# Output weights moved from the first MLP pass into gaps of the projections' plan, and half of the T forms put in the places of the token forms

## The chip, the cores and the metric

The kernel runs on one core of a Trainium2 chip. The time is device microseconds (us) of one execution. The engines are PE (TensorE, with PEld for its weight loads), DVE (VectorE), ACT (ScalarE), POOL (GpSimd) and SP (SyncE, which issues the DMAs here). Each works through its own queue of instructions in order.

## The reference

For 2048 tokens of 640 numbers, the result is the input, plus a linear attention of its layer norm, plus an MLP of its layer norm:

```python
xn = _layernorm(x)
return x + _A_ref(xn, A_wqkv, A_w_phi, A_wo) + _B_ref(xn, B_w1, B_b1, B_w2, B_b2)

# _A_ref: 32 heads of 20
q, k, v = split(x @ wqkv)
pq, pk = q @ w_phi, k @ w_phi                    # per head
phi = concat(softmax(p), softmax(-p))            # for q and for k
kv, z = phi_k^T @ v, sum over tokens of phi_k
o = (phi_q @ kv) / (phi_q @ z + 1e-6)
return o @ wo
# _B_ref
return gelu(layernorm(x) @ w1 + b1) @ w2 + b2    # 640 -> 1728 -> 640
```

## The kernel before

All matmuls work on pairs of numbers. A float32 operand is split into a high part (an ACT copy that rounds it) and a low part (the rest, by a subtract on POOL or DVE), and a product is three matmuls: high by high, high by low, low by high (`mm3`, lines 68 to 71). Tokens come in four blocks `b` of 512, hidden units in 14 chunks of 128, taken in seven groups `g` of two.

The stages in order of time, by the trace: the first MLP pass over blocks 0 and 1 for all groups, up to about 225 us; then the projections of q, k and v with the feature maps and phi_k^T v, up to about 447 us; then the MLP over blocks 2 and 3 with the attention beside it; then the product with `wo`.

**The first pass** (`Mlp.passes`) runs, for each group and block, the first layer (two chunks, 30 matmuls), then the second layer of the pass before it (five columns of 6 matmuls, each read out of its bank by a DVE add, L338). Between two passes the next weight chunk is split (`take`; L60 on ACT, L63 on POOL or DVE; the last, half-wide chunk 13 by L60, L63 and L271 to L275). After every 3 matmuls `Mlp.tick` runs one step of a generator, `beside`. In this pass that is `prep()`, which prepares what later stages read. Its last part is a list of `events`, each a tick number and a step, sorted by tick. An event says when a step is written into its engine's queue; there it runs when what stands before it is done and its data are there. The events of before:

- For the ten tiles (c, b) of the tokens of blocks 2 and 3 (c of 5 rows of 128, b of 2 blocks): `load` of a 128x512 tile `xq` (four buffers; L795), `centred` on POOL at tick +0 (L798), `scaled` on DVE at +3 (L801), `hi` on ACT at +5 (L805) and `lo` on DVE at +7 (L809). `hi` and `lo` write the two halves of a tile `t`, of which there are two buffers; two DMAs store them (L811). The tiles follow each other every 5 ticks.
- *Token forms* (`form_sub` on POOL L835, `form_hi` on ACT L839, `form_lo` on DVE L843, stores L846): differences of halves of tiles, for a scheme that saves matmuls in the projections. For block 2 they lie in `temps[:4]`, four 128x512 pieces of the memory of `acc2`: the forms in the first two, their high parts in the other two.
- *T forms* (`combine` on POOL L821, then `hi`, L805, and `combined_lo` on DVE L826, with one store of 512 KB, L827): differences of tiles, four for each `q` in (0, 1), for a like scheme in the later MLP. They use the same two buffers `t`.
- *Output weights* (`wo_load` L855, `wo_hi` on ACT L858, `wo_lo` on POOL L861 with two stores L863): the first 512 of the 640 columns of `wo`, in five blocks `kc` of 128 rows, at ticks 46, 49, 52, 97 and 100, with `wo_hi` 8 and `wo_lo` 10 ticks later. They lie in `temps`, `spare` and `own["t"]`.
- `raw_sums` from tick 122 (DVE L918, POOL L921): sums of weight blocks in `temps`.

DVE, ACT, POOL and PE keep the order in which the program writes their instructions. SP's order is chosen by the framework.

**The projections** are written by a planner, `Plan` (from line 1200). Each `add` names an engine, a duration, a function that emits the instructions, and what must be done before. `run()` places the operations one after another, each at the earliest time by its priority, and emits an operation when it is placed. `plan_pair` plans two tiles of 128 tokens; inside, `plan_wo` (L1529) plans the last 128 columns of `wo` in three parts, each a load, an ACT copy (L1541), a POOL subtract (L1544) and stores (L1548). `next_forms` loads 1 MB of token forms for the next pair (L1197). `store_phi` stores turned features (L1178) from five places `turns`, which are used in turn.

Of the kernel before, what the change touches and what calls it, by code (L numbers as in the profile page):

```python
# [8 lines left out]
F32 = mybir.dt.float32  # L9
F32R = mybir.dt.float32r  # L10
AF = mybir.ActivationFunctionType
ALU = mybir.AluOpType
# [3 lines left out]
P = 128  # L16
S, D, F, H, DH = 2048, 640, 1728, 32, 20
KC = D // P
# [27 lines left out]
def f(ap):  # L46
    return ap.bitcast(F32)
# [3 lines left out]
def tile_kernel(ctx: ExitStack, tc: tile.TileContext, x, xT, wkT, wqT, wv, wphi, wo, w1, b1, w2, b2,  # L51
# [715 lines left out]
    def prep():  # L767
# [32 lines left out]
        def scaled(c, b):  # L800
            nc.vector.tensor_tensor(xs[c, b], xs[c, b], mr[b][:, 1], op=ALU.mult)  # L801

        def hi(*at):
            hls[at] = gp.tile([P, 2, 512], F32R, name="t")
            nc.scalar.activation(hls[at][:, 0], xs[at], AF.Copy)  # L805

        def lo(*at):
            hl = hls.pop(at)
            nc.vector.tensor_tensor(hl[:, 1], xs[at], f(hl[:, 0]), op=ALU.subtract)  # L809
            for p in range(2):  # L810
                nc.sync.dma_start(y_dram[at[1] - 2][p][:, at[0], :], f(hl[:, p]))  # L811
# [11 lines left out]
        def combined_lo(q, i):  # L823
            at = combined(q, i)[0]
            hl = hls.pop(at)
            nc.vector.tensor_tensor(hl[:, 1], xs[at], f(hl[:, 0]), op=ALU.subtract)  # L826
            nc.sync.dma_start(t_dram[q][:, i], f(hl))  # L827

        def form_sub(b, q, i):
            w = 512 if b == 2 else 2 * P  # L830
# [20 lines left out]
        wos = {}  # L851

        def wo_load(kc):
            wos[kc] = [(temps[0], temps[1]), (temps[2], temps[3]), (spare[0], own["t"])][kc % 3]
            nc.sync.dma_start(wos[kc][0], wo[kc * P:(kc + 1) * P, :512])  # L855

        def wo_hi(kc):
            nc.scalar.activation(wos[kc][1].bitcast(F32R), wos[kc][0], AF.Copy)  # L858

        def wo_lo(kc):  # L860
            nc.gpsimd.tensor_tensor(wos[kc][0].bitcast(F32R), wos[kc][0], wos[kc][1], op=ALU.subtract)  # L861
            for w, wd in zip(wos[kc][::-1], wo_dram):
                nc.sync.dma_start(wd[:, kc, :512], w)  # L863

        for kc, at in enumerate((46, 49, 52, 97, 100)):
            for after, step in ((0, wo_load), (8, wo_hi), (10, wo_lo)):
                events.append((at + after, len(events), step, (kc,)))

        for n, step in enumerate(raw_sums(0, temps)):
            events.append((122 + 3 * n, len(events), step, ()))  # L870
        base = 8
        for q in range(3):
            tiles = [(c, b) for c in range(2 * q, min(2 * q + 2, KC)) for b in range(2, 4)]
            for n, at in enumerate(tiles):
                late = 6 * (at == (KC - 1, 3))
                for after, step in ((-6, load), (0, centred), (3, scaled), (5 + late, hi), (7 + late, lo)):
                    events.append((base + 5 * n + after, len(events), step, at))
            if q < 2:
                for b, at, his, los in ((2, 14, (25, 27), (27, 29)), (3, 19, (29, 31), (31, 33))):
                    for i in range(4):  # L880
                        events.append((base + at + i, len(events), form_sub, (b, q, i)))
                    for i in range(2):
                        events.append((base + his[i], len(events), form_hi, (b, q, i)))
                        events.append((base + los[i], len(events), form_lo, (b, q, i)))
            base += 5 * len(tiles) + (9 if q < 2 else 5)
            if q < 2:
                for n, i in enumerate((0, 2, 1, 3)):
# [312 lines left out]
    class Plan:  # L1200
# [31 lines left out]
            for op, t in zip(self.ops, last):  # L1232
                op[4] = t

        def run(self):

            self.latest()
            engines = ("PE", "ACT", "DVE", "POOL", "SP")
# [4 lines left out]
            rest = []  # L1243
            while any(left.values()):
                best = None
                for e, ops in left.items():
# [15 lines left out]
                op[0] = e  # L1262
                free[e] = op[5] = at + op[1][e]
                if left["PE"] or e == "PE":
                    op[2][e]()
# [125 lines left out]
        if (t, 1 - n) in got:  # L1391
            plan_features(t, "k", j, got[t, 0][0], got[t, 1][0])

    at, got, wo_done = {}, {}, []
    yts = {}

    def plan_pair(t):
# [78 lines left out]
    def next_forms(t):  # L1476
        if t < 12:
            yts[t + 2] = load_forms(t + 2)
        else:
            for q in range(2):  # L1480
                for p in range(2):
                    nc.sync.dma_start(f(wkv_[p][:, 2 * q, 512:1024]), s_dram[:, q, p])

    def plan_sums():
# [34 lines left out]
                late[1 + i][:] = way  # L1519

        done = splits(1, ts, ways1, (plan.add("ACT", 0.0, place, *done, *made),))
        w_ready["s1"] = (*w_ready["s1"], plan.add("SP", 3.5, lambda: next_forms(0), *done))
        return thirds

# [1 line left out]
        acc[2] = own["a"].tile([P, KC, 512], F32, name="acc2")  # L1526
        load_acc(2)

    def plan_wo(n, *after):  # L1529

        ks, cols = slice(2 * n, min(2 * n + 2, KC)), slice(512, D)
        raw = {}

        def load():
            r = rp.tile([P, D], F32, name="r2")
            w = (ks.stop - ks.start) * P
            raw.update(lo=r[:, :w], hi=r[:, 320:320 + w])
            nc.sync.dma_start(raw["lo"].rearrange("p (c n) -> p c n", n=P), wo[ks.start * P:ks.stop * P, cols].rearrange("(c p) n -> p c n", p=P))

        def hi():  # L1540
            nc.scalar.activation(raw["hi"].bitcast(F32R), raw["lo"], AF.Copy)  # L1541

        def lo():
            nc.gpsimd.tensor_tensor(raw["lo"].bitcast(F32R), raw["lo"], raw["hi"], op=ALU.subtract)  # L1544

        def store():
            for w, wd in zip((raw["hi"], raw["lo"]), wo_dram):
                nc.sync.dma_start(wd[:, ks, cols], w.rearrange("p (c n) -> p c n", n=P))  # L1548

        a = plan.add("SP", 0.7, load, *after, *wo_done)  # L1550
        b = plan.add("ACT", 0.4, hi, a)
        c = plan.add("POOL", 0.7, lo, b)
        wo_done[:] = [plan.add("SP", 1.4, store, c)]

    def first_weights():
        nonlocal mlp
# [30 lines left out]

    w1t = w2t = late = None
    w_ready = {}
    thirds = plan_sums()  # L1590
    for n, (t, i) in enumerate(((0, 0), (0, 1), (1, 1), (0, 2), (0, 3), (1, 0), (1, 2), (1, 3))):
        plan_part(t, i, n % 3)
# [23 lines left out]
    for b, op in stores:  # L1616
        for m in range(4):
            stored = plan.add("SP", 2.8, lambda b=b, m=m: store_phi(b, m), op, at[4 * b + 4, m] if b else op)
            if m < 3:
                turned[4 * b + 4][3] = (*turned[4 * b + 4][3], stored)  # L1620
    ptile.n = n
    over = plan.run()
    order.close()
    for step in over:
        step()
# [601 lines left out]
```

## Time and profile before

| | |
|---|---|
| median of three runs | 709.65 us |
| lowest and highest | 708.47 and 710.87 us |
| the profiled execution | 707.67 us |
| its span, first to last instruction | 705.9 us |
| mean granted PE clock | 0.995 |
| DMA | 123.37 MB, mean 175 GB/s |

A row of the profile names a line, an engine and an operation, what it writes and reads by the program's names, and times. A bracket such as `[3.18 <-DMA t<-t]` means that the engine was idle for 3.18 us before this instruction, and what ended it: here a DMA that read or wrote a tile `t`. "Granted clock" is the share of full speed at which PE ran. PE's matmuls overlap, so their lengths add up to more than the time they take.

### The profile page before, as it was taken

Reading aid. Unit: us, or ns where it says so; the run is one execution under the profiler, and the core shown is the slowest. Engines: PE = TensorE matmul, PEld = TensorE weight load, DVE = VectorE, ACT = ScalarE, POOL = GpSimd, SP = SyncE. Lnnn points to the kernel's source line nnn. Section 1 sums busy time; section 2 is a strip of 40 time slices with the busy share of each in tenths; the row PEclk is TensorE's granted clock in tenths of the full one; section 3 lists DMA queues with packets and bytes.
Section 4 is the critical chain, followed back from the end, with each engine's and each line's share of the span. In section 5 each row is a group of like instructions: output and inputs, shape, how many; then the busy total and the mean of one; then the engine's idle time right before and its main releaser. Section 6 shows DMA issues by size and latency. Waiting matters only on the chain.

```text
span 705.9 us, 9957 instructions
## 1 busy us (share of the span) xinstructions
PE 691.2 (98%) x3295; PEld 579.6 (82%) x3295; DVE 544.3 (77%) x912; ACT 376.6 (53%) x644; POOL 516.1 (73%) x390
## 2 busy tenths in 40 slices
PE   8999999997899999999999999999999999999997
PEld 7888888876677888888888888888888888888886
DVE  7878774877667788788888888848688697789783
ACT  6444564444343455455454465657677667659350
POOL 3717585879539779979979999848689997577930
PEclk9999999999989999999999999999999999999999
DMA  9815867597845213384370564984355648871222
GB/s 325 248 59 176 251 190 250 205 302 260 263 165 179 86 59 125 125 211 162 96 186 0 159 150 148 313 254 116 124 141 162 186 145 290 284 275 65 75 75 105
DMA packets 78202, 123.37 MB, mean 175 GB/s; under 512 B 8502, under 2 KB 41942, under 8 KB 75758
## 3 DMA queue, kind: packets, MB, share of 16 engines
q1 hardware_dynamic: 75670, 120.62, 53.4%
q10 hardware_dynamic: 2480, 2.11, 0.9%
q8 instruction: 26, 0.43, 0.3%
q14 instruction: 26, 0.21, 0.1%
HBM read 79.76 MB, written 42.94 MB: 174 GB/s over the span
## 4 chain that ended last, share of the span: by engine, by line
PE 82%; DVE 6%; DMA 5%; POOL 3%; issue 2%; ACT 2%; SPq 0%; DVEq 0%; POOLq 0%; ACTq 0%
PE bank L1044 17%; PE bank L69 15%; PE bank L71 15%; PE bank L70 15%; PE bank L1416 8%; PE bank L1157 3%; PE bank L1420 2%; PE bank L650 2%; POOL xq L798 1%; PE bank L1768 1%; PE bank L1769 1%; DMA t<-t 1%; DMA f<-xq 1%; PE bank L556 1%; DVE acc L843 1%
## 5 line engine op out<-in xcount | busy, mean ns | idle before, releaser
L69 PE MATMUL bank<-m,w 128*128 128x512 f32 x288 | 113.9, 396 | 3.7 <-DVE acc L338 3.7
L70 PE MATMUL bank<-m,w 128*128 128x512 f32 x288 | 112.4, 390 | 0.0
L71 PE MATMUL bank<-m,w 128*128 128x512 f32 x266 | 103.8, 390 | 0.0
L69 PE MATMUL bank<-y,w 128*128 128x512 f32 (+1 forms) x256 | 99.6, 389 | 0.0
L70 PE MATMUL bank<-y,w 128*128 128x512 f32 (+1 forms) x256 | 98.8, 386 | 0.0
L71 PE MATMUL bank<-y,w 128*128 128x512 f32 (+1 forms) x246 | 95.1, 387 | 1.2 <-POOL w L63 1.2
L63 POOL TENSOR_TENSOR w<-r,w 128x640 fp32r<-128x640 f32 x29 | 49.5, 1719 | 30.2 <-ACT w L60 25.6
L69 PEld LDWEIGHTS bank<-m,w 128*128 128x128 f32 x288 | 54.4, 189 | 17.3 <-DVE acc L338 5.7
L1044 PE MATMUL bank<-wkh,y 128*128 128x320 f32 (+1 forms) x240 | 63.1, 337 | 0.0
L70 PEld LDWEIGHTS bank<-m,w 128*128 128x128 f32 x288 | 54.2, 188 | 10.8
L71 PEld LDWEIGHTS bank<-m,w 128*128 128x128 f32 x266 | 50.1, 188 | 10.7
L1044 PE MATMUL bank<-w,y 128*128 128x512 f32 x240 | 57.5, 391 | 0.0
L69 PEld LDWEIGHTS bank<-y,w 128*128 128x128 f32 x256 | 48.1, 188 | 10.4 <-ACT bank L1836 0.3
L70 PEld LDWEIGHTS bank<-y,w 128*128 128x128 f32 x256 | 48.1, 188 | 9.5
L71 PEld LDWEIGHTS bank<-y,w 128*128 128x128 f32 x246 | 46.2, 188 | 11.1 <-POOL w L63 1.6
L338 DVE TENSOR_TENSOR acc<-bank,acc 128x512 f32<-128x512 f32 x70 | 46.4, 680 | 8.5 <-PE bank L334 5.0
L1762 POOL TENSOR_TENSOR e<-e,m 128x512 fp32r<-128x512 f32 x28 | 41.1, 1468 | 15.4 <-ACT m L1761 14.4
L1044 PEld LDWEIGHTS bank<-w,y 128*128 128x128 f32 x240 | 44.4, 188 | 8.5
L1097 POOL TENSOR_TENSOR m<-m,w 128x1280 f32<-128x1280 f32 x16 | 41.3, 2584 | 11.3 <-DVE w L1090 10.0
L1084 DVE TENSOR_REDUCE sm<-m 128x64 f32<-128x1280 f32 x32 | 47.1, 1472 | 2.9 <-ACT m L1079 2.6
L1138 ACT ACTIVATE v<-bank,rs_all 128x132 fp32r<-128x132 f32 (+2 forms) x48 | 19.6, 443 | 52.4 <-PE bank L1044 52.1
L1076 POOL TENSOR_TENSOR m<-m,mx 128x640 f32<-128x640 f32 x32 | 40.9, 1279 | 8.3 <-DVE mx L1066 4.1
(311 smaller groups left out, 1827.9 us busy)
## 6 DMA issues: line engine op xcount, KB each, us to landing
r<-in_w SPq DMA_DIRECT2D x52, 320.0 KB
e<-e SPq DMA_DIRECT2D x40, 256.0 KB
e<-acc SPq DMA_DIRECT2D x52, 160.0 KB
w<-f SPq DMA_DIRECT2D x6, 1024.0 KB
t<-t SPq DMA_DIRECT2D x8, 512.0 KB
acc<-in_xT SPq DMA_DIRECT2D x3, 1280.0 KB
tf<-t SPq DMA_DIRECT2D x2, 1536.0 KB
xb<-in_x SPq DMA_DIRECT2D x8, 320.0 KB
```

The source lines that it names most:

```text
L63: eng.tensor_tensor(lo, src, f(hi), op=ALU.subtract)
L69: nc.tensor.matmul(ps, lh, rh, start=first, stop=False, **kw)
L70: nc.tensor.matmul(ps, lh, rl, start=False, stop=False, **kw)
L71: nc.tensor.matmul(ps, ll, rh, start=False, stop=last, **kw)
L338: nc.vector.tensor_tensor(acc[b][:, m, :], pw, acc[b][:, m, :], op=ALU.add)
L1044: nc.tensor.matmul(ps, lh[:, kc, c], rh[:, kc], start=n == 0, stop=n == 3 * KC - 1)
L1076: subs[n, t] = nc.gpsimd.tensor_tensor(ep[:, :, s], a, b, op=ALU.subtract)
L1084: nc.vector.tensor_reduce(sm, e.rearrange("p a (h f) -> p (a h) f", f=DH), axis=AX, op=ALU.add)
L1097: nc.gpsimd.tensor_tensor(e3, e3, w.unsqueeze(2).to_broadcast([P, 2 * H, DH]), op=ALU.mult)
L1157: nc.tensor.matmul(kvp[g // 2][:, (g % 2) * 240:(g % 2) * 240 + 240].rearrange("p (i c) -> p i c", i=2), v[:, g * VS:(g + 1) * VS], ft[:, ...
L1416: nc.tensor.matmul(ps, left(yn, pl, q), right(w, pr, q), start=first and q == 0 and n == 0, stop=False, skip_group_check=True)
L1762: mlp.after(1, lambda: nc.gpsimd.tensor_tensor(pl, e, f(ph), op=ALU.subtract))
```

## The change

- The events of `wo` leave the first pass: five loads, ACT copies, POOL subtracts and pairs of stores.
- `plan_wo` leaves the plan. In its place five *pieces* (`wo_piece`), one for each block of 128 rows and all 640 columns, are placed after the plan is finished: `run()` first collects what it planned in `seq`, with times. Then, for each piece, it looks on each engine that a step may use for the first gap that is long enough after the step before it (SP is taken as free), and puts the step there; the subtract goes to POOL (1.9) or DVE (1.0), whichever can begin first. At the end all is emitted in order of planned time. The raw block lies in `r2`, its high part in a place of `turns` that isn't in use: the fifth, once the second set of sums is split, the fourth and third, after their features are stored.
- Of the four T forms of each `q`, the second and the fourth in order write into `temps[0:2]` and `temps[2:4]` rather than into a buffer `t`. All T forms are stored by two DMAs of 256 KB instead of one.
- Ticks: `scaled` at +4 instead of +3, `hi` at +7 instead of +5, `lo` at +9 instead of +7; the subtracts of the token forms one tick later.

```diff
-        def hi(*at):
-            hls[at] = gp.tile([P, 2, 512], F32R, name="t")
-            nc.scalar.activation(hls[at][:, 0], xs[at], AF.Copy)
+        def hi(*at, place=None):
+            hl = gp.tile([P, 2, 512], F32R, name="t") if place is None else place
+            hls[at] = [hl[:, p] for p in range(2)] if place is None else [z.bitcast(F32R) for z in place]
+            nc.scalar.activation(hls[at][0], xs[at], AF.Copy)
...
-            nc.sync.dma_start(t_dram[q][:, i], f(hl))
+            for p in range(2):
+                nc.sync.dma_start(t_dram[q][:, i, p], f(hl[p]))
...
-        for kc, at in enumerate((46, 49, 52, 97, 100)):
-            for after, step in ((0, wo_load), (8, wo_hi), (10, wo_lo)):
-                events.append((at + after, len(events), step, (kc,)))
...
-                for after, step in ((-6, load), (0, centred), (3, scaled), (5 + late, hi), (7 + late, lo)):
+                for after, step in ((-6, load), (0, centred), (4, scaled), (7 + late, hi), (9 + late, lo)):
...
-                for b, at, his, los in ((2, 14, (25, 27), (27, 29)), (3, 19, (29, 31), (31, 33))):
+                for b, at, his, los in ((2, 15, (25, 27), (27, 29)), (3, 20, (29, 31), (31, 33))):
...
-                    for after, step in ((0, combine), (3, lambda q, i: hi(*combined(q, i)[0])), (5, combined_lo)):
+                    place = temps[n - 1:n + 1] if n % 2 else None
+                    for after, step in ((0, combine), (3, lambda q, i, place=place: hi(*combined(q, i)[0], place=place)), (5, combined_lo)):
...
+            for begin, steps in pieces:
+                at = begin() if callable(begin) else begin
+                for wait, emit, ways in steps:
+                    places = []
+                    for e, took in ways.items():
+                        t = at
+                        for s, end in sorted((s[0], s[2]) for s in seq if s[1] == e != "SP" and s[2] > at):
+                            if s >= t + took:
+                                break
+                            t = max(t, end)
+                        places.append((t, t + took, e))
+                    t, end, e = min(places)
+                    seq.append((t, e, end, lambda e=e, emit=emit: emit(e)))
+                    at = end + wait
+                self.filled = at
+            for s in sorted(seq, key=lambda s: s[0]):
+                s[3]()
...
-        if t < 8:
-            plan_wo(t // 2 - 1, at[t, 2])
...
+    def wo_piece(kc):
+
+        raw, place = {}, (4, 4, 3, 3, 2)[kc]
+
+        def load(_):
+            raw.update(lo=rp.tile([P, D], F32, name="r2"), hi=turns[place].rearrange("p c n -> p (c n)")[:, :D])
+            nc.sync.dma_start(raw["lo"], wo[kc * P:(kc + 1) * P, :])
+
+        def hi(_):
+            nc.scalar.activation(raw["hi"].bitcast(F32R), raw["lo"], AF.Copy)
+
+        def lo(e):
+            (nc.vector if e == "DVE" else nc.gpsimd).tensor_tensor(raw["lo"].bitcast(F32R), raw["lo"], raw["hi"], op=ALU.subtract)
+
+        def store(_):
+            for w, wd in zip((raw["hi"], raw["lo"]), wo_dram):
+                nc.sync.dma_start(wd[:, kc, :], w)
+
+        return (lambda: max(plan.filled, kept[place][5] + 3.0) if kc else kept[4][5]), \
+            [(5.5, load, {"SP": 0.7}), (0.2, hi, {"ACT": 0.8}), (0.2, lo, {"POOL": 1.9, "DVE": 1.0}), (3.0, store, {"SP": 0.7})]
...
-    over = plan.run()
+    over = plan.run([wo_piece(kc) for kc in range(KC)])
```

More of the change, by code (lines that the diff above doesn't have):

```diff
@@ L801, in scaled @@
             nc.vector.tensor_tensor(xs[c, b], xs[c, b], mr[b][:, 1], op=ALU.mult)
-        def hi(*at):
-            hls[at] = gp.tile([P, 2, 512], F32R, name="t")
-            nc.scalar.activation(hls[at][:, 0], xs[at], AF.Copy)
+        def hi(*at, place=None):
+            hl = gp.tile([P, 2, 512], F32R, name="t") if place is None else place
+            hls[at] = [hl[:, p] for p in range(2)] if place is None else [z.bitcast(F32R) for z in place]
+            nc.scalar.activation(hls[at][0], xs[at], AF.Copy)
         def lo(*at):
             hl = hls.pop(at)
-            nc.vector.tensor_tensor(hl[:, 1], xs[at], f(hl[:, 0]), op=ALU.subtract)
+            nc.vector.tensor_tensor(hl[1], xs[at], f(hl[0]), op=ALU.subtract)
             for p in range(2):
-                nc.sync.dma_start(y_dram[at[1] - 2][p][:, at[0], :], f(hl[:, p]))
+                nc.sync.dma_start(y_dram[at[1] - 2][p][:, at[0], :], f(hl[p]))
         def combined(q, i):
@@ L825, in combined_lo @@
             hl = hls.pop(at)
-            nc.vector.tensor_tensor(hl[:, 1], xs[at], f(hl[:, 0]), op=ALU.subtract)
-            nc.sync.dma_start(t_dram[q][:, i], f(hl))
+            nc.vector.tensor_tensor(hl[1], xs[at], f(hl[0]), op=ALU.subtract)
+            for p in range(2):
+                nc.sync.dma_start(t_dram[q][:, i, p], f(hl[p]))
         def form_sub(b, q, i):
@@ L849, in prep @@
         form_places = {2: temps[:4], 3: [z[:, o:o + 2 * P] for z in (spare[0], own["t"]) for o in (0, 2 * P)]}
[L851 to L863, printed above, removed]
-        for kc, at in enumerate((46, 49, 52, 97, 100)):
-            for after, step in ((0, wo_load), (8, wo_hi), (10, wo_lo)):
-                events.append((at + after, len(events), step, (kc,)))
         for n, step in enumerate(raw_sums(0, temps)):
@@ L1233, in latest, with run @@
                 op[4] = t
-        def run(self):
+        def run(self, pieces):
             self.latest()
@@ L1242, in run @@
                     left[e].append((n, op))
-            rest = []
+            seq, rest = [], []
             while any(left.values()):
@@ L1264, in run @@
                 if left["PE"] or e == "PE":
-                    op[2][e]()
+                    seq.append((at, e, op[5], op[2][e]))
                 else:
                     rest.append(op[2][e])
+            for begin, steps in pieces:
[15 more added lines that the diff above has]
+                s[3]()
             return rest
@@ L1392, in plan_part @@
             plan_features(t, "k", j, got[t, 0][0], got[t, 1][0])
-    at, got, wo_done = {}, {}, []
+    at, got = {}, {}
     yts = {}
@@ L1521, in plan_sums @@
         done = splits(1, ts, ways1, (plan.add("ACT", 0.0, place, *done, *made),))
+        kept[4] = done[-1]
         w_ready["s1"] = (*w_ready["s1"], plan.add("SP", 3.5, lambda: next_forms(0), *done))
@@ L1527, in load_acc2 @@
         load_acc(2)
[L1529 to L1540, printed above, removed]
+    def wo_piece(kc):
[4 more added lines that the diff above has]
+        def hi(_):
             nc.scalar.activation(raw["hi"].bitcast(F32R), raw["lo"], AF.Copy)
-        def lo():
-            nc.gpsimd.tensor_tensor(raw["lo"].bitcast(F32R), raw["lo"], raw["hi"], op=ALU.subtract)
-        def store():
+        def lo(e):
+            (nc.vector if e == "DVE" else nc.gpsimd).tensor_tensor(raw["lo"].bitcast(F32R), raw["lo"], raw["hi"], op=ALU.subtract)
+        def store(_):
             for w, wd in zip((raw["hi"], raw["lo"]), wo_dram):
[L1548 to L1553, printed above, removed]
+                nc.sync.dma_start(wd[:, kc, :], w)
+        return (lambda: max(plan.filled, kept[place][5] + 3.0) if kc else kept[4][5]), \
+            [(5.5, load, {"SP": 0.7}), (0.2, hi, {"ACT": 0.8}), (0.2, lo, {"POOL": 1.9, "DVE": 1.0}), (3.0, store, {"SP": 0.7})]
     def first_weights():
@@ L1589, in tile_kernel @@
     w_ready = {}
+    kept = {}
     thirds = plan_sums()
@@ L1620, in tile_kernel @@
                 turned[4 * b + 4][3] = (*turned[4 * b + 4][3], stored)
+            if (b, m) in ((0, 3), (1, 3)):
+                kept[3 - b] = stored
     ptile.n = n
-    over = plan.run()
+    over = plan.run([wo_piece(kc) for kc in range(KC)])
     order.close()
```

## The prediction

> **What bounds the kernel now.** I read the page first, then the time of each engine by stretches, then who keeps TensorE waiting, then the timelines of the engines around each such wait.
>
> ```profile
> span 705.9 us, 9957 instructions
> PE 691.2 (98%) x3295; PEld 579.6 (82%) x3295; DVE 544.3 (77%) x912; ACT 376.6 (53%) x644; POOL 516.1 (73%) x390
> ```
>
> TensorE (PE) sets the time: it idles 14.7 us in all. The change adds and removes no matmul, so its effect is only in those idle times, in the clock, and in new idle times. The next rows are stretches (start:end, length, busy time and instructions of PE, PEld, DVE, ACT, POOL, then granted clock, DMA share, GB/s).
>
> ```profile
> 160.00:200.00 40.00, 32.78 (x132) 25.93 (x131) 26.30 (x35) 15.27 (x28) 24.87 (x20) 0.92 0.72 242
> ...
> 195.00:200.00 5.00, 5.00 (x12) 3.81 (x13) 2.98 (x6) 1.91 (x4) 0.00 (x0) 0.50 0.40 157
> ...
> 225.00:435.00 210.00, 210.00 (x1091) 182.44 (x1090) 180.62 (x299) 105.67 (x168) 182.23 (x129) 1.00 0.41 122
> ```
>
> The worst stretch, 160 to 200 us, is the first MLP pass with the layout work beside it, which is what the diff edits; it also holds the only drop of the clock, to 0.50. The projections, 225 to 435 us, where the new work goes, have no idle PE at all. Who PE waited for from 100 to 260 us (total, times, longest), and the PE rows that price it (start, length):
>
> ```profile
> PE bank L69 <- DVE acc L338: 3.7, 4, 2.6
> PE bank L314 <- DVE w L63: 3.4, 1, 3.4
> PE bank L71 <- POOL w L63: 1.2, 1, 1.2
> PE bank L333 <- POOL m L321: 0.2, 1, 0.2
> ```
>
> ```profile
> 145.02 0.39 PE L71 MATMUL bank<-y,w 128*128 128x512 f32 x1
> ...
> 151.82 0.39 PE L71 MATMUL bank<-m,w 128*128 128x512 f32 x1
> 152.43 0.50 PE L69 MATMUL bank<-m,w 128*128 128x512 f32 x1 [0.22 <-DVE acc L338]
> ...
> 161.48 0.50 PE L71 MATMUL bank<-y,w 128*128 128x512 f32 x1 [1.18 <-POOL w L63]
> ...
> 171.43 0.50 PE L69 MATMUL bank<-m,w 128*128 128x512 f32 x1 [2.63 <-DVE acc L338]
> ...
> 194.87 0.79 PE L314 MATMUL bank<-y,w 128*128 128x512 f32 x1 [3.41 <-DVE w L63]
> ...
> 200.67 0.40 PE L69 MATMUL bank<-m,w 128*128 128x512 f32 x1
> ```
>
> From 145.02 to 151.82 lie 30 steps: 0.227 us each when PE runs on. A row's length is 0.39, so each idle time loses itself and 0.16 more: from 151.82 to 152.43 the step is 0.61, that is 0.38 lost where 0.22 is shown. Seven waits with 8.5 us idle lose 8.5 + 7 x 0.16 = 9.6 us. From 194.87 to 200.67 there are 13 steps, which at 0.227 would be 2.95 us and took 5.80: the half clock loses another 2.85. **Lost in the first pass: 12.5 us.**
>
> Why PE waits there:
>
> ```profile
> 149.24 0.63 ACT L805 ACTIVATE t<-xq 128x512 fp32r<-128x512 f32 x1 [3.18 <-DMA t<-t]
> ...
> 158.26 0.63 ACT L805 ACTIVATE t<-xq 128x512 fp32r<-128x512 f32 x1 [1.98 <-DVE xq L801]
> 158.80 1.35 ACT L60 ACTIVATE w<-r 128x640 fp32r<-128x640 f32 x2
> ...
> 167.63 0.63 ACT L805 ACTIVATE t<-xq 128x512 fp32r<-128x512 f32 x1 [3.77 <-DVE xq L801]
> 168.17 0.64 ACT L293 ACTIVATE bank<-bank,b1t 128x512 f32<-128x512 f32 x1
> ...
> 189.11 0.63 ACT L805 ACTIVATE t<-xq 128x512 fp32r<-128x512 f32 x1 [6.00 <-DMA t<-t]
> 193.30 0.63 ACT L805 ACTIVATE t<-xq 128x512 fp32r<-128x512 f32 x1 [3.56 <-DMA t<-t]
> 193.84 0.45 ACT L60 ACTIVATE w<-r 128x320 fp32r<-128x320 f32 x1
> ```
>
> ```profile
> 183.25 4.67 DMA f<-acc
> ...
> 187.97 0.33 SPq L966
> ...
> 188.39 4.81 DMA t<-t
> ```
>
> ```profile
> 153.90 1.27 POOL L861 TENSOR_TENSOR acc<-acc 128x512 fp32r<-128x512 f32 x1 [4.93 <-ACT acc L858]
> 155.13 1.30 POOL L798 TENSOR_TENSOR xq<-xq,m 128x512 f32<-128x512 f32 x1
> 156.39 1.29 POOL L861 TENSOR_TENSOR acc<-acc 128x512 fp32r<-128x512 f32 x1
> ...
> 163.36 1.30 POOL L861 TENSOR_TENSOR acc<-acc,s 128x512 fp32r<-128x512 f32 x1
> ```
>
> Two causes. First, the high part of a T form (ACT, L805) waits for a t buffer whose 512 KB store has not landed; there are two such buffers for four T forms. Behind it in ACT's queue stand the GELU (L293) or the next weights' split (L60). At 189.11 and 193.30 this holds the split of weight chunk 13 at 193.84, and PE stops until 194.87. The store that it waits for was itself behind SP's L966, held until a form store (4.67 us) had landed. The wait of 3.18 us at 149.24 makes the stops near 152 and 154 in the same way. Second, POOL: the low part of an output-weight block (L861) sits at 153.90 waiting 4.93 us for ACT, with the centring L798 behind it; that makes DVE and then ACT (158.26) late, behind which the weights' split (158.80) is what PE waits for at 161.48. The next L861s put the same chain off again: ACT at 167.63, the GELU at 168.17, DVE, and PE at 171.43.
>
> **The change, part by part.** *Output weights out of the first pass.* Five times a load, an ACT copy (0.63 like L805's), a POOL subtract (five of about 1.3 us, 6.5 us in all), two stores go. The three subtracts quoted and the 4.93 us wait are directly on the chain of the stops at 161 and 171, 1.34 + 2.79 = 4.1 us. POOL without them reaches L798 up to 3 us earlier, as soon as its load is there. The split of the weights then has its time: PE needs the low part 17 steps, 3.9 us, after the pass begins, and ACT takes 0.68 (half of the row at 158.80) and POOL about 1.6 (1.3 by 640/512), so 1.6 us are to spare. What is late next: POOL, busy 19.1 of the 20 us below, still has 16.5 without the two subtracts that start and end in them, 83%, so I leave 1.0 us of stops.
>
> ```profile
> 155.00:175.00 20.00, 16.19 (x70) 12.55 (x69) 13.64 (x18) 8.42 (x14) 19.10 (x18) 1.00 0.79 296
> ```
>
>  It can't go below nothing, since only work is taken away; at worst all 4.1 stay. Moving hi, lo and scaled one or two ticks later (a tick is 3 matmuls, 0.68 us) lets POOL be up to 0.7 us later before DVE, and 1.4 us before ACT, is blocked; what it delays, the stores of y and T, is read only after 225 us.
>
> *Half of the T forms in temps.* Forms 2 and 3 no longer take a t buffer, so forms 0 and 1 each find one whose low part was emitted 13 and 16 ticks, 9 and 11 us, before. The stops near 152 and 154 (0.38 + 0.75) and at 194.87 (3.57 + 2.85) should go: 7.5 us. A new wait comes: form 2's high part goes to the place of the token form's low part, whose store is emitted 9 ticks, 6.1 us, before. DVE's subtract takes 0.7 to 1.8, the store 4.67, so ACT waits at most about 0.8 us (or none); behind it stand a GELU whose result is read 30 matmuls (6.8 us) later, and the split at 193.84, three forms away. Cost nothing; if that cover were gone, 0.8 us per form. Eight T stores become sixteen: 8 x 0.33 us of SP, against 15 issues that leave it.
>
> *End of the pass.* The raw sums waited for the stores of the last output weights out of the same places. That goes, and with it the last two stops, 0.28 and 0.20 idle, 0.8 lost.
>
> *Output weights in the projections.* Three pieces there before (128 or 256 columns) become five of 640 columns: ACT about 0.68 each (half of the row at 158.80), DVE about 0.84 (the shortest L801 below, by 640/512) or POOL 1.6, two stores, one load. SP gets 15 issues for 9; behind them stand the loads of token forms. They are put in gaps of the plan, but the queues run in order and the gaps are the planner's.
>
> ```profile
> L801 DVE TENSOR_TENSOR xq<-xq,m x10: 674/1488/2051, 121.5 to 206.8; 128x512 f32<-128x512 f32 x10
> ...
> L1109 POOL TENSOR_TENSOR w<-m,w x9: 2957/2961/2987, 262.8 to 393.2; 128x1280 fp32r<-128x1280 f32 x9
> L1109 DVE TENSOR_TENSOR w<-m,w x7: 1429/1482/1909, 251.8 to 438.9; 128x1280 fp32r<-128x1280 f32 x7
> ...
> ACT m L1318 <- PE bank L1416: 23.6, 23, 2.8
> ```
>
> ACT waits for PE up to 2.8 us at a time, 23 times, so a copy of 0.68 has room; DVE is busy 86% and POOL 87% of 225 to 435. The same kind of subtract in this stage, L1109 on DVE, took at most 1909 - 1429 = 0.48 us longer than its shortest. So a piece's subtract lasts up to 1.3 us in a gap planned at 1.0: 5 x 0.3 = 1.5 us late at most if nothing absorbs it, and none if it does. A load that lands late would hold ACT more; the planned wait is 5.5 us, and the slowest store quoted took 4.81. A gain isn't excluded, since the plan itself changes when the old pieces leave it, but PE has no idle time to give. I take 0.5, between 0 and 3.
>
> Rule and trace. The idle of 3.41 us brings the clock to 0.50, the idle of 2.63 us doesn't (0.227 steps go on). The Trainium skill, "TensorE: Matmul & The Clock Gate", Part 1: The HAM clock gate, says that the array falls to half clock after an idle window of about 3.4 us and comes back after as long of work; the trace agrees on the fall. By its figure for the return the half clock would cost an estimated 1.7 us, and the sum would be 1.1 smaller; the measured 2.85 is used.
>
> **Sum:** 12.5 lost, less 1.0 that stays, less 0.5 given back: 11.0 us. The profiled execution took 707.67 us (span 705.9 and 1.8 around it); it would take 696.7. The median is 709.65, 2.0 above it; minus 11.0 that is **698.6**.
>
> **Rivals.** *A form store takes the t store's place.* ACT waits for f stores instead, and chunk 13's split stays late. For it: 4.67 us to land with SP held up at L966. Against it: 6.1 us between. The stop at 194.87 would stay, 6.4 us: gain 4.6, **705.1**. Chance 0.16.
>
> *POOL stays the bound of the pass.* At 83% with its splits in bunches, the stops at 161 and 171 stay, 4.1 us instead of the 1.0 that I left (3.1 more): gain 7.9, **701.7**. For it: 19.1 of 20 us busy from 155 to 175. Against it: three of those pieces of work go. Chance 0.12.
>
> *Slower: the subtracts collide in the projections.* A piece's DVE subtract is held for a whole POOL instruction, 2.96 us (L1109), in a gap of 1.0, DVE's bank moves come late, and PE, without slack, pays 2.96 + 0.84 - 1.0 = 2.8 us for each of five pieces: 14 us. Result 709.65 - 12.5 + 1.0 + 14 = **712.2**. It turns slower once a piece costs PE more than 2.3 us. For it: DVE's L801 went from 674 to 2051 ns beside a busy POOL. Against it: L1109's 0.48 in this very stage, and no PE idle there now. Chance 0.08. The Trainium skill, "SBUF — State Buffer", Who interferes with whom, states this as a rule: a DVE instruction with two SBUF inputs and a GpSimd one that reads SBUF exclude each other, and the second fully blocks; L801's 1.38 us longer, about one POOL subtract, agrees, L1109 hardly.
>
> *It doesn't do what it says:* PE comes 11 us earlier to the projections and is held there by work that hasn't moved, so that all is given back; about **709**. Only the absence of PE waits after 225 us speaks against it. Chance 0.06.
>
> **The numbers.** Forecast 0.58 (its own range 695.5 to 701). Faster by over 0.3% (2.1 us, about what a measurement of this kernel can tell): 0.58 + 0.16 + 0.12 = 0.86; the same 0.06; slower 0.08. The low end is all 12.5 gained and 1.7 for scatter (the runs span 708.47 to 710.87): 695.5. The high end takes in the first two rivals: 705.5.
>
> **Right or wrong.** Right: in the new profile no PE wait on L63 or L338 over 1 us before the projections, a clock of 1.00 throughout, no L805 waiting for t<-t, and PE without idle in the projections, which begin at about 213 us instead of 225. Wrong: L805 waiting for DMA of acc (the forms' places), POOL L63 still releasing PE, or PE waits in the projections released by ACT or DVE lines of the bank moves.

## The result and the profile after

| | before | after |
|---|---|---|
| median | 709.41 us (6 runs) | 697.13 us (6 runs) |
| lowest and highest | 708.22 and 710.87 us | 695.98 and 699.88 us |
| ratio, 95% interval | | 0.9833 (0.9812 to 0.9855) |
| profiled execution | 707.67 us | 695.98 us |
| its span | 705.9 us | 694.2 us |

The kernel became 12.3 us faster. In the code after, some lines have other numbers: `hi` is L806 (it was L805), `lo` L810 (L809), a T form's `lo` L827 (L826), a token form's L845 (L843), the projections' matmul L1029 (L1044). The pieces are L1536 (load), L1539 (ACT), L1542 (subtract) and L1546 (stores).

The page of after: PE is busy 686.4 us of a span of 694.2, so it idles 7.8 us where it idled 14.7.

```profile
span 694.2 us, 9954 instructions
...
PE 686.4 (99%) x3295; PEld 578.0 (83%) x3295; DVE 545.5 (79%) x916; ACT 376.4 (54%) x641; POOL 511.0 (74%) x383
```

The stretches of after (columns as in the prediction). From 160 to 200 us PE has no idle time and the clock is 1.00; the projections, from 213 us, have none either. Between 40 and 560 us, 120 to 160 is the only stretch of 40 us with idle PE; the rest of the 7.8 us lies in the first 40 us, at the end and a little near 570 us.

```profile
120.00:160.00 40.00, 38.04 (x167) 30.85 (x166) 32.34 (x39) 17.08 (x29) 29.45 (x24) 1.00 0.66 217
160.00:200.00 40.00, 40.00 (x178) 32.99 (x177) 36.49 (x48) 17.79 (x31) 24.67 (x21) 1.00 0.66 221
...
213.00:425.00 212.00, 212.00 (x1099) 184.06 (x1098) 183.36 (x305) 109.85 (x173) 185.21 (x128) 1.00 0.45 141
```

Whom PE waited for in the whole of after (total, times, longest): the waits on L63 are gone, and one on L338 is left between the start and the attention (L584, L1767).

```profile
PE bank L69 <- DVE acc L338: 1.9, 1, 1.9
PE bank L584 <- POOL m L582: 1.3, 1, 1.3
PE bank L187 <- DVE xb L173: 0.3, 1, 0.3
PE bank L1767 <- DVE acc L1781: 0.2, 1, 0.2
```

Where the time came from can be read from two marks on PE's timeline that both kernels have: the first matmul of the MLP, and the first of the projections. First before, then after.

```profile
19.16 0.40 PE L69 MATMUL bank<-y,w 128*128 128x512 f32 x1
...
224.95 0.39 PE L1044 MATMUL bank<-wkh,y 128*128 128x512 f32 x1
```

```profile
18.48 0.40 PE L69 MATMUL bank<-y,w 128*128 128x512 f32 x1
...
137.38 0.39 PE L71 MATMUL bank<-m,w 128*128 128x512 f32 x1
139.71 0.50 PE L69 MATMUL bank<-m,w 128*128 128x512 f32 x1 [1.94 <-DVE acc L338]
...
213.25 0.39 PE L1029 MATMUL bank<-wkh,y 128*128 128x512 f32 x1
```

Between the marks lie 205.79 us before and 194.77 after: 11.02 less. From the second mark to the end of the span it is 705.9 - 224.95 = 480.95 and 694.2 - 213.25 = 480.95, the same. The remaining 0.68 us lie ahead of the first mark, where the two kernels do the same; PE waits there for the first normed tokens (L187). They are scatter and no gain of the change: the experiment below that alters only SP's order in the kernel before has its first mark at 18.46. From the second mark to the end, executions scatter too: the three kernels here with the plan of before took 480.56, 480.95 and 481.21 us, the five with the pieces in their gaps 480.95 to 481.29. So the change's gain is in the first pass, nothing beyond this scatter is given back in the projections, and one stop of 1.94 us at 139.71 is new.

ACT in the first pass of after: the T forms of the second set, two of them now into `acc` (the memory of `temps`), and the split of weight chunk 13 (L60 on 128x320).

```profile
175.99 0.63 ACT L806 ACTIVATE t<-xq 128x512 fp32r<-128x512 f32 x1 [0.62 <-POOL xq L822]
...
178.37 0.62 ACT L806 ACTIVATE acc<-xq 128x512 fp32r<-128x512 f32 x1
178.89 0.62 ACT L806 ACTIVATE t<-xq 128x512 fp32r<-128x512 f32 x1
180.58 0.63 ACT L806 ACTIVATE acc<-xq 128x512 fp32r<-128x512 f32 x1 [1.07 <-POOL xq L822]
181.12 0.46 ACT L60 ACTIVATE w<-r 128x320 fp32r<-128x320 f32 x1
```

None of the four waits for a store, and the split that stood at 193.84 stands at 181.12. POOL without the output weights' subtracts:

```profile
153.92 1.30 POOL L798 TENSOR_TENSOR xq<-xq,m 128x512 f32<-128x512 f32 x1 [4.03 <-DMA xq<-in_xT]
155.79 1.29 POOL L798 TENSOR_TENSOR xq<-xq,m 128x512 f32<-128x512 f32 x1 [0.57 <-DMA xq<-in_xT]
157.04 4.00 POOL L63 TENSOR_TENSOR w<-r,w 128x640 fp32r<-128x640 f32 x2
```

L798 now begins as soon as its load is there, 1.21 and 1.85 us earlier than before (155.13 and 157.64 there, the second not shown), and the split 2.56 us earlier (159.60, not shown either).

### The profile page after: what moved, and what is told of

It is laid out like the page before. It is cut to its first block, busy times and chain, and to the rows that moved or that the text cites. A ratio compares the mean times of both kernels' runs of the same rounds, so it can differ in the third digit from the quotient of the medians.

```text
span 694.2 us, 9954 instructions
## 1 busy us (share of the span) xinstructions
PE 686.4 (99%) x3295; PEld 578.0 (83%) x3295; DVE 545.5 (79%) x916; ACT 376.4 (54%) x641; POOL 511.0 (74%) x383
## 4 chain that ended last, share of the span: by engine, by line
PE 94%; DVE 3%; ACT 1%; issue 0%; DMA 0%; DVEq 0%; ACTq 0%
PE bank L69 19%; PE bank L71 18%; PE bank L70 18%; PE bank L1029 17%; PE bank L1418 8%; PE bank L1142 3%; PE bank L1422 2%; PE bank L650 2%; PE bank L1767 1%; PE bank L1768 1%; PE bank L556 1%; PE bank L314 1%; PE bank L334 1%; PE bank L315 1%; PE bank L333 1%; DVE st L139 0%
## 5 line engine op out<-in xcount | busy, mean ns | idle before, releaser
L63 POOL TENSOR_TENSOR w<-r,w 128x640 fp32r<-128x640 f32 x29 | 49.1, 1708 | 30.6 <-ACT w L60 19.4
L1029 PE MATMUL bank<-wkh,y 128*128 128x320 f32 (+1 forms) x240 | 63.1, 337 | 0.0
L1029 PE MATMUL bank<-w,y 128*128 128x512 f32 x240 | 57.5, 391 | 0.0
L338 DVE TENSOR_TENSOR acc<-bank,acc 128x512 f32<-128x512 f32 x70 | 46.9, 681 | 11.5 <-PE bank L71 6.1
L1029 PEld LDWEIGHTS bank<-w,y 128*128 128x128 f32 x240 | 44.4, 188 | 8.5
L1061 POOL TENSOR_TENSOR m<-m,mx 128x640 f32<-128x640 f32 x32 | 42.8, 1338 | 8.7 <-DVE mx L1051 4.2
```

The costliest lines, as they stand in the source:

```text
L63: eng.tensor_tensor(lo, src, f(hi), op=ALU.subtract)
L338: nc.vector.tensor_tensor(acc[b][:, m, :], pw, acc[b][:, m, :], op=ALU.add)
L1029: nc.tensor.matmul(ps, lh[:, kc, c], rh[:, kc], start=n == 0, stop=n == 3 * KC - 1)
L1061: subs[n, t] = nc.gpsimd.tensor_tensor(ep[:, :, s], a, b, op=ALU.subtract)
```

## The experiments

Each had its own runs of the kernel before beside it; a ratio is to those. "The theory" is mostly the prediction's, unless the expectation says otherwise.

**The two parts alone.** First without the T forms' places:

```diff
-                    place = temps[n - 1:n + 1] if n % 2 else None
+                    place = None
```

> All four T forms go back to the two t buffers; the rest of the change stays. Theory (two separate causes that add up): the stops that came from POOL, near 161 and 171 us, stay away (4.1 us, and 0.8 at the end of the pass), and the stops behind the T forms come back: near 152 and 154 us (1.1 us) and before weight chunk 13 (3.6 us and 2.9 us of half clock). About 697.1 + 7.5 = 704.6 us, ACT waiting for DMA of t<-t, a clock below 1 in one stretch. Rival (one cause: the output weights' traffic made the T stores land late): no such waits without that traffic, 697 to 699 us and full clock.

Measured: 700.6 us (4 runs), ratio 0.9868 (0.9835 to 0.9902), between the two expectations. Its PE timeline has two stops, and soon after each of them eight steps or so of 0.43 us, the half clock:

```profile
139.85 0.51 PE L69 MATMUL bank<-m,w 128*128 128x512 f32 x1 [2.16 <-DVE acc L338]
140.18 0.60 PE L70 MATMUL bank<-m,w 128*128 128x512 f32 x1
...
143.56 0.42 PE L69 MATMUL bank<-m,w 128*128 128x512 f32 x1
...
190.28 0.50 PE L314 MATMUL bank<-y,w 128*128 128x512 f32 x1 [1.60 <-DVE w L63]
...
191.42 0.63 PE L315 MATMUL bank<-y,w 128*128 128x512 f32 x1
...
194.83 0.40 PE L70 MATMUL bank<-m,w 128*128 128x512 f32 x1
```

The stop before chunk 13 stays, but 1.60 us long rather than 3.41, and the stops near 152 and 154, which the prediction laid to the T forms, are gone without the T forms' part. (With no stop at 139 ahead of them they come back, as a later experiment shows.)

Then the T forms' part alone: the kernel before with two of four T forms in other places. As `temps` is taken by the output weights, the first set used `spare` and `own["t"]`, one output-weight block moved from tick 52 to 56, and the last two took other places (the T forms are stored by two DMAs each, as in the change).

```diff
-        for kc, at in enumerate((46, 49, 52, 97, 100)):
+        for kc, at in enumerate((46, 49, 56, 97, 100)):
...
+                    place = None if n % 2 == 0 else (spare[0], own["t"]) if q == 0 else temps[n - 1:n + 1]
```

> The kernel before, with the T forms' second and fourth in other places than the t buffers (for the first half in the two other scratch pieces, for the second half in temps) and stored by two DMAs; the output weights stay in the first pass (block 2 is loaded 4 ticks later, blocks 3 and 4 use other scratch pieces) and the ticks are those of before. Theory (two separate causes): the stops near 152 and 154 us and before chunk 13 go (7.5 us), those behind POOL near 161 and 171 us stay (4.1 us): about 709.4 - 7.5 = 701.9 us. Rival (the output weights are the one cause): under 3 us are gained, 707 us or more, and ACT still stands before chunk 13's split.

Measured: 703.77 us, ratio 0.9915 (0.9882 to 0.9948). The stop before chunk 13 is gone. PE's waits in the first pass are now all on L338, but for one of 0.2 us; one ACT row tells where the longest new wait on ACT comes from, and three PE rows show the longest stop, with steps of 0.43 us soon after it:

```profile
PE bank L69 <- DVE acc L338: 6.2, 4, 2.6
```

```profile
148.54 0.63 ACT L806 ACTIVATE acc<-xq 128x512 fp32r<-128x512 f32 x1 [5.98 <-DMA f<-acc]
```

```profile
172.34 0.50 PE L69 MATMUL bank<-m,w 128*128 128x512 f32 x1 [2.62 <-DVE acc L338]
...
173.40 0.63 PE L69 MATMUL bank<-m,w 128*128 128x512 f32 x1
173.83 0.63 PE L70 MATMUL bank<-m,w 128*128 128x512 f32 x1
```

Here a T form does wait for a token form's store, 5.98 us, with the GELU at 149.07 behind it: the first rival's mechanism, in the places that this experiment had to use for the first set. In the changed kernel, whose `temps` are free, it is absent. So this run is no clean price of the T forms. Of the two stops that the prediction laid to POOL it has the one near 171 us (2.62 us at 172.34) and not the one near 161, but two longer ones stand ahead of that, 0.98 us at 153.43 and 1.75 at 156.85.

The gains alone are 8.7 us (709.34 - 700.6) and 5.6 (709.34 - 703.77), 14.3 together against 12.3 for both at once. Their intervals are 6.9 to 11.7 and 3.7 to 8.4, and in the profiled executions it is the other way round: from mark to mark the two are 5.8 and 3.4 us shorter than before, 9.2 together, and both at once 11.0. So whether the parts overlap in sum is not shown. At the one stop before chunk 13 they do: 3.41 us with neither part, 1.60 with the first, none with the second.

**The ticks.** The stop at 139.71 was not in the kernel before, where the step to the same matmul, at 138.32, took 0.25 us. DVE there, before and then after:

```profile
135.79 1.27 DVE L809 TENSOR_TENSOR t<-xq,t 128x512 fp32r<-128x512 f32 x1
136.98 0.68 DVE L63 TENSOR_TENSOR m<-bank,m 128x512 fp32r<-128x512 f32 x1
137.59 0.68 DVE L338 TENSOR_TENSOR acc<-bank,acc 128x512 f32<-128x512 f32 x1
```

```profile
134.33 1.22 DVE L801 TENSOR_TENSOR xq<-xq,m 128x512 f32<-128x512 f32 x1
137.44 0.69 DVE L63 TENSOR_TENSOR m<-bank,m 128x512 fp32r<-128x512 f32 x1 [1.88 <-ACT m L60]
138.04 1.01 DVE L810 TENSOR_TENSOR t<-xq,t 128x512 fp32r<-128x512 f32 x1
138.97 0.68 DVE L338 TENSOR_TENSOR acc<-bank,acc 128x512 f32<-128x512 f32 x1
```

Before, the low part (L809) ran ahead of the hidden units' subtract (L63) while ACT was busy. Two ticks later it stands behind L63 and ahead of L338, which frees the bank that PE waits for: L338 starts 1.38 us later than before, 0.46 of them because L63 itself starts later and 0.92 with L810 in between. PE, by its earlier start, comes 0.68 us sooner. Together that is the 2.1 us that the stop costs (2.33 - 0.227). Two runs put ticks back, one everywhere and one in the first half only; the second is this edit:

```diff
-                for after, step in ((-6, load), (0, centred), (4, scaled), (7 + late, hi), (9 + late, lo)):
+                sc, h, l = ((3, 5, 7) if q == 0 else (4, 7, 9))
+                for after, step in ((-6, load), (0, centred), (sc, scaled), (h + late, hi), (l + late, lo)):
```

> The change with the ticks of before (scaled at +3, hi at +5, lo at +7, token forms one tick earlier) everywhere. Theory (the one stop left, 1.9 us idle at 139.7 us, was made by the later ticks: the last tile's low part now stands on DVE between the hidden unit's low part and the bank reads): it goes, 2.1 us less, 695.0 us, and no other stop comes. Rival (the later ticks are needed, since POOL is late in the second half): stops near 160 to 172 us come back, 699 to 701 us.

All back (the token forms' tick too): 696.52 us, ratio 0.981 (0.9782 to 0.9838). The stop at 139 is gone, and two others are there instead:

```profile
159.02 0.50 PE L71 MATMUL bank<-y,w 128*128 128x512 f32 x1 [0.77 <-POOL w L63]
...
167.71 0.50 PE L69 MATMUL bank<-m,w 128*128 128x512 f32 x1 [1.37 <-DVE acc L338]
```

> The change with scaled, hi and lo at the ticks of before for the first four tiles alone, those around the stop at 139.7 us; later tiles and all token forms keep the later ticks. Theory (the later ticks made that stop): 2.1 us less, 695.0 us, by either view of the second half. Rival (the stop comes from POOL's and DVE's load there and not from the ticks): 697 us and a stop of 1 to 2 us near 138 to 140 us.

The first half alone: **694.8 us** (694.34 to 695.51, 5 runs), ratio 0.9785 (0.9757 to 0.9813). It is the fastest kernel of this study. No stop near 139, and its second mark is the earliest but for one experiment below:

```profile
211.71 0.39 PE L1030 MATMUL bank<-wkh,y 128*128 128x512 f32 x1
```

Its first mark is at 18.53, so its pass takes 193.18 us, 1.59 less than the changed kernel's. The later ticks cost that in the first half and are needed in the second, where the kernel with all ticks back (the token forms' too) stops twice and takes 195.19.

**The T forms' places once more,** on this faster kernel, where no stop at 139 lies between (`place = None` as in the first experiment):

> The changed kernel with the old ticks in the first half of the first pass, and all four T forms of a set in the two t buffers. Theory: with the output weights gone the T forms' places are worth only the stop before weight chunk 13, 1.6 us idle with the half clock behind it, 3.3 to 3.6 us in all: about 698.2, of which PE waits for DVE's L63 1.6 us near 188 us. Rival, as the prediction sized it: 7.5 us less the stops near 152 and 154, 6.4: about 701. Other rival: the places are worth nothing once the pass is on time: 694.8.

Measured: 697.68 us (4 runs), ratio 0.9848 (0.9822 to 0.9874), 2.9 over the median of the kernel that it was made from; from mark to mark it takes 196.65 us, 3.5 more. PE, then ACT:

```profile
153.31 0.50 PE L69 MATMUL bank<-m,w 128*128 128x512 f32 x1 [1.33 <-DVE acc L338]
...
155.40 0.50 PE L69 MATMUL bank<-m,w 128*128 128x512 f32 x1 [0.42 <-DVE acc L338]
...
189.04 0.50 PE L314 MATMUL bank<-y,w 128*128 128x512 f32 x1 [1.36 <-DVE w L63]
```

```profile
150.12 0.63 ACT L806 ACTIVATE t<-xq 128x512 fp32r<-128x512 f32 x1 [4.29 <-DMA xq<-in_xT]
...
187.47 0.63 ACT L806 ACTIVATE t<-xq 128x512 fp32r<-128x512 f32 x1 [4.26 <-DMA t<-t]
```

The stop before chunk 13 is back, 1.36 us and with no half clock after it, and so are the two stops near 153 and 155, with the GELU (L293, 150.66) behind a T form's `hi` that waited 4.29 us. That `hi` reads what POOL combines, not a fresh load; the load named is only what came last by the profile, and that it waited for a buffer `t` is inferred from the form before it. The sum agreed with the theory, its parts didn't. And the prediction had rightly laid the stops near 152 and 154 to the T forms: in the first experiment the stop at 139 had covered them.

**SP's order.** The prediction said that the store of a T form was itself held up behind SP's L966. The kernel before, with L966 issued after the last T store:

```diff
-            nc.sync.dma_start(t_dram[q][:, i], f(hl))
+            loads["t"] = nc.sync.dma_start(t_dram[q][:, i], f(hl)).ins
...
-            nc.sync.dma_start(raw, wv[kc * P:(kc + 1) * P, :VF * H])
+            with tc.issue_after(loads["t"]):
+                nc.sync.dma_start(raw, wv[kc * P:(kc + 1) * P, :VF * H])
```

> The kernel before, with one change of order: the loads of the value weights are issued on SP only after the last store of a T form, so that SP no longer stands at the first of them (it waited there for a form store) ahead of the second T store. Theory (what made chunk 13's split late is the chain form store, SP, T store): that store is issued some 2.6 us earlier, the stop of 3.4 us shrinks to about 0.8 us and the half clock goes: 709.3 - 2.6 - 2.9 = 704 us. Rival (the T store's own transfer and the two buffers set it): the stop stays at 3 us or more, 708 to 710 us.

Measured: 707.68 us (10 runs), ratio 0.9986 (0.997 to 1.0001): no change that can be told. PE's two longest waits in the first pass:

```profile
PE bank L69 <- DVE acc L338: 3.9, 3, 2.6
PE bank L314 <- DVE w L63: 2.6, 1, 2.6
```

The wait before chunk 13 goes from 3.41 to 2.58 us, and the half clock stays. The hold-up explains 0.83 us of that stop. For the rest, the T store now issued 2.5 us earlier (185.89 for 188.39) still held the last `hi` until 192.75 (193.30 before); with two of four forms in other places, above, the stop was gone. The pass as a whole is no shorter, 206.03 us from mark to mark: 0.5 us more went ahead of 108 us, where the edit changes nothing, and the half clock lasted longer.

**The pieces in the projections.** The edit took the search for gaps away, so that each step stands where its data are planned to be ready (DVE, the shorter way, then takes every subtract). It was run on the changed kernel and on the faster one:

```diff
-                        for s, end in sorted((s[0], s[2]) for s in seq if s[1] == e != "SP" and s[2] > at):
-                            if s >= t + took:
-                                break
-                            t = max(t, end)
```

> The change, with each step of an output-weight piece put at the time when the step before it is done, whether or not the engine has a gap there (all five subtracts then go to DVE). Theory (the projections have room enough on ACT and DVE before PE is touched, gaps or not): 697.1 us, not over 698, and no PE wait in the projections. Rival (the search for gaps is what hides the pieces): each of five pieces costs PE 0.6 to 1.3 us, 700 to 703 us, with PE waits released by the lines that move banks.

> The changed kernel with the old ticks in the first half of the first pass (694.8, no stop near 139 us), and without the search for gaps: each output-weight piece stands where its load ends in the plan. Theory: the gaps are worth the 1.7 us that the projections took longer without them; the projections take 482.6 us, the kernel about 696.5, and PE waits once for about 1.3 us near 243 us. Rival: the 1.7 us were scatter or came from the different start of the projections; 694.8.

Measured on the changed kernel: 699.59 us, ratio 0.9888 (0.984 to 0.9935). From the second mark (215.57) to the end it took 482.63 us, 1.7 more than 480.95; the mark itself is 2.3 us later, mostly by the stop near 140, 2.34 us idle there and with half clock behind it, which this edit doesn't touch. On the faster kernel: 696.5 us (5 runs), ratio 0.9828 (0.9807 to 0.985), from the mark (211.77) to the end 482.53 against 481.29 without the edit, and one PE wait over 0.15 us in the projections, 1.26 us at 242.79:

```profile
PE bank L1415 <- DVE m L1315: 1.3, 1, 1.3
```

The gaps are worth 1.2 to 1.7 us by these traces, beside a spread of 0.7 among the eight kernels above. The second edit kept them and did each piece's copy and subtract twice, the extra subtract into free memory:

```diff
-            nc.scalar.activation(raw["hi"].bitcast(F32R), raw["lo"], AF.Copy)
+            for _ in range(2):
+                nc.scalar.activation(raw["hi"].bitcast(F32R), raw["lo"], AF.Copy)
...
+            for scratch in (turns[place].rearrange("p c n -> p (c n)")[:, D:2 * D], raw["lo"]):
+                eng.tensor_tensor(scratch.bitcast(F32R), raw["lo"], raw["hi"], op=ALU.subtract)
```

> The change, with the ACT copy and the subtract of each output-weight piece in the projections done twice (the extra subtract goes to a free place), while the plan still counts each once: 5 x 0.73 us more on ACT and 5 x about 0.8 us more on DVE or POOL, outside any planned gap. Theory (the pieces cost PE nothing since there is room): 697.1 us, not over 698. Rival (the subtracts collide and only just fit): 1.5 us for each piece, about 704 us, with PE waits in the projections.

> The changed kernel with the old ticks in the first half of the first pass, and each output-weight piece's copy and subtract done twice, so that it holds ACT 0.74 us and DVE 0.76 us longer than planned. Theory: the projections have little room outside the planned gaps; they take 483.3 us, the kernel about 697.2. Rival: PE's queue rides over that; 694.8. If each piece's overrun of 0.76 us on DVE went to PE whole, 3.8 us: 698.6.

On the changed kernel: 701.71 us, ratio 0.9907 (0.9871 to 0.9942); from the mark (214.30) to the end of the span (697.6) 483.3 us, 2.35 more. On the faster kernel: 696.04 us (5 runs), ratio 0.9834 (0.9808 to 0.986); its second mark is at 210.84, the earliest of all, and from there to the end (693.9) it is 483.06, 1.77 over 481.29. Its longest PE wait in the projections:

```profile
PE bank L1419 <- ACT m L1321: 1.0, 1, 1.0
```

So five pieces with their work done twice cost 1.8 to 2.4 us in all, about 0.4 each. They overran the plan by more than the 0.75 us that the expectations reckoned with: four of the second subtracts were on DVE and took 1.77 to 2.87 us, not 0.76, as POOL was already at work. The longest, on DVE and then POOL beside it:

```profile
243.73 2.87 DVE L1546 TENSOR_TENSOR r<-r,et 128x640 fp32r<-128x640 f32 x1
```

```profile
242.95 2.97 POOL L1083 TENSOR_TENSOR m<-m,w 128x1280 f32<-128x1280 f32 x1 [1.18 <-DVE w L1076]
```

POOL's ends at 245.92, and DVE's 0.68 us after that. This is the mechanism of the prediction's slower rival, at about 0.4 us a piece rather than its 2.8. That the median on the changed kernel is 701.71 is not explained by this: the profiled execution, 699.5, is the lowest of the four, and the others have no trace.

## Why the prediction was right, and where it was not

**The sum.** Forecast 698.6, measured 697.13. The forecast gain was 11.0, and the trace shows 11.02 from the first mark to the end. The difference of 1.5 is the 0.68 us ahead of the first mark, and that the median of after lies 1.15 us over its profiled execution (697.13 - 695.98), not 2.0. Of the three terms of the gain each was off, and the errors cancel; that they meet so closely is luck:

**What is lost in the first pass** was put at 12.5. The faster kernel's pass is 205.79 - 193.18 = 12.6 us shorter, and still has a stop of 0.49 us idle, so it was 13.3 or so; the faster kernel with doubled pieces, whose first pass has no such stop in its profiled execution, took 192.32, 13.5 less. The term left out is the step after each stop: 0.33 instead of 0.227 us, seven times 0.1.

**What stays** was put at 1.0 of stops made by POOL. PE's waits on POOL's split went entirely. Instead a stop stays that the prediction didn't have, 2.1 us at 139.71. The step that failed is "Moving hi, lo and scaled one or two ticks later ... lets POOL be ... later": it named what the move gives and looked, for its price, only at what is stored late, not at where the moved subtract lands in DVE's queue. The order there made 0.92 of the 1.38 us by which L338 came late. The forecast of "no PE wait on L63 or L338 over 1 us" was wrong by this one stop, and 694.8 us is the kernel without it.

**The split, 4.1 for POOL and 7.5 for the T forms,** was wrong though the sum held. The output weights alone (with the ticks) are worth 8.7 us, the T forms alone 5.6, each within some 2.4 either way, and on the faster kernel, with the output weights gone, the T forms 3.5 of the first pass. The stop before chunk 13 is 3.41 us with both causes, 1.60 or 1.36 without the output weights (and with the later ticks), and none without the shared buffers: the buffers make it, and the output weights lengthen it. I gave each stop to one cause by its nearest wait, and a stop can have two. Whether it is the traffic of `wo` or POOL's time that lengthens it was not tried apart.

**"The store that it waits for was itself behind SP's L966"** was true in the trace and mattered little: 0.83 of 3.41 us.

**No new wait on the token forms' stores:** right for the places of the changed kernel; all four `hi` of the second set begin without one. Two earlier `hi` do wait for a DMA of those places, 2.7 us of ACT's time, which the prediction had named as a sign of being wrong, but with no PE stop behind:

```profile
ACT t L806 <- DMA t<-acc: 2.7, 2, 2.2
```

The rows that wait (148.22 and 157.66, 0.43 and 2.24 us) write to a buffer `t`; why a store out of `temps` should hold them is not shown. A wait of 5.98 us on a token form's store, with other places, is what the experiment with the T forms alone met. The cover is the time since the last store out of a place, so it has to be reckoned anew for each place.

**The projections** were put at 0.5, between 0 and 3: it was 0.0, within the scatter given above. A piece's subtract was expected to last 0.84 to 1.3 us on DVE and took 0.76 in four pieces, less than the 1.0 planned; the fifth ran on POOL (1.58). It did collide with POOL, as the slower rival had it, but the other way round. POOL's L1061 in after, and L1076, the same instruction in before (count, then lowest/median/highest ns):

```profile
L1061 POOL TENSOR_TENSOR m<-m,mx x32: 1274/1279/1904, 223.5 to 425.0; 128x640 f32<-128x640 f32 x32
```

```profile
L1076 POOL TENSOR_TENSOR m<-m,mx x32: 1272/1279/1289, 235.2 to 436.4; 128x640 f32<-128x640 f32 x32
```

And one of three such places on DVE and on POOL in after:

```profile
322.81 0.76 DVE L1542 TENSOR_TENSOR r<-r,acc 128x640 fp32r<-128x640 f32 x1
```

```profile
322.80 1.90 POOL L1061 TENSOR_TENSOR m<-m,mx 128x640 f32<-128x640 f32 x1
```

The two begin together; DVE's takes its usual time and POOL's 0.62 us longer. The rule weighed in the prediction (the Trainium skill, "SBUF — State Buffer", Who interferes with whom) says that the shared ports are an exclusive lock and that the order of issue decides who blocks. The trace agrees with the exclusion: here POOL waits, and in the doubled pieces above, where POOL's instruction began 0.78 us before, DVE does. Which of the two was issued first here is not shown, with starts 0.01 us apart. POOL had the room: no PE wait follows.

**The clock.** 1.00 in all stretches of the profiled execution, as forecast; of the six executions of after, three have a mean of 0.997 or 0.998, so the half clock is not gone for good. The price of 2.85 us belonged to that stop of before; most other half clocks here were shorter, below.

## What to carry to other kernels

A stop can have two causes, so the parts of a change are priced by doing each alone, not by sharing out the stops among them. When a step is moved to a later tick, look at what it now stands behind and ahead of in its queue; an instruction that used to fill an idle time can come to stand ahead of the one that frees PE. Work put into a finished plan cost nothing here while it fitted gaps with room to spare: 0.0 us with gaps, 1.2 to 1.7 without, and about 0.4 us for each piece whose work was doubled.

## What the runs showed of the hardware that was not expected

The half clock does not go by the length of the stop alone. The plainest pair is the stop near 171 us on L338: 2.63 us in the kernel before, with steps of 0.23 us after it, and 2.62 us in the experiment with the T forms alone, with steps of 0.43. It also came after 1.60 and 2.16 us of idle PE (the first experiment) and 2.34 (the one without gaps, on the changed kernel) and 2.58 (SP's order), and not after 1.94 (after, at 139.71) and 1.36 (189.04 above). In the first experiment it lasted from 140.18 to 143.56 and from 191.42 to 194.83, 3.4 us each, and the two beginnings are 51.24 us apart, 15 times 3.416. The Trainium skill, "TensorE: Matmul & The Clock Gate", Part 1: The HAM clock gate, tells of a free-running window of 3413 ns; the duration and this distance agree with that, its idle time of about 3.4 us before the clock falls does not. The prediction's "the trace agrees on the fall" rested on two stops of before, and these runs don't bear it out. With a window that runs on its own, the same stop may or may not cost a further 1.6 us or so, by where it falls (eight steps at 0.43 instead of 0.227). The six executions of the changed kernel, one and the same program, fit that: the three with a mean clock of 1.000 took 695.98 to 696.98 us, the three with 0.997 or 0.998 took 697.28 to 699.88, while the kernel without the stop at 139 took 694.34 to 695.51 at 0.999 or 1.000. That the window's place decides remains an inference; only one execution of each has a trace.
